# A recurrence with its products evicted to borrowed tiles, its second to fourth operand sets loaded earlier, and a new step order

## The chip, the cores and the metric

The kernel runs on one core of a Trainium2 chip. Its time is the device time of one execution in microseconds (us); below, the median of three runs. A profiled execution gives the trace. The engines are TensorE (PE in the profile; PEld are its weight loads), VectorE (DVE), ScalarE (ACT), GpSimd (POOL) and SyncE (SP), which issues most DMA transfers.

## The reference

Inputs r, k, v, w, a, b of 4 batches, 8 heads, 768 steps, 40 features run through a recurrence; its output is the input of two further layers.

```
for t in range(S):
    y[t]  = r[t] @ state
    Sa    = state @ a[t]
    state = state * w[t] - outer(Sa, b[t]) + outer(v[t], k[t])
u   = x + ((x^T @ U) @ V)^T;  x = u + relu(u @ w_ch1) @ w_ch2      (320 -> 1280 -> 320)
out = top-2 of 4 causal attention heads of width 64, each weighted by its gate, @ wo
```

## The kernel before

The recurrence (L58 to L486, the first 372.6 us) works on 12 chunks of 64 steps and 2 pairs of batches: 24 units u, unit u = chunk u // 2, pair u % 2. Operands come in 16 sets j of 1.05 MB (128 rows of 2057 floats: 512 columns each of two key-like factors and of a, and 521 of w). Two sets (j = 2m, 2m + 1) hold three units: set 2m + r holds unit 3m + r in 80 of its rows, and half of unit 3m + 2, the guest, in the 40 other rows that are used. The slots of sets 0 and 1 are tiles of their own (ldt), those of sets 2 and 3 lie in not yet used parts of the output tiles (x).

The order of the work on all engines is written out by hand: ORDER_R is a string, each letter runs one generator up to its next yield (L477). Each engine works through its own instructions in that order; semaphores do the rest. The letters:

- d, scaled(j): VectorE makes the scans P (L195) and er (L203), the product bkt (L208) and F (L216); then SyncE issues unit u's rows ga (L219), two transfers. Four steps a set.
- g, sent(j): three pairs of transfers by SyncE (L164), which bring the guest's rows of P, bkt and F into P_g, bkt_g and the guest's ga. P_g and bkt_g exist once.
- m, loads (L177): one load of a set, or of a piece; before, sets 1 to 3 come in three pieces (a, b, c).
- f, front(u): TensorE transposes P (pt) and bkt (pb) and multiplies bkt by ga (pg, L255, two halves); ScalarE evicts. The halves of pg are evicted over bkt itself (L258), so the eviction waits for every reader of bkt. Then GpSimd copies four blocks into lx (L263), cuts masks into ga (sel, L266) and copies m21 (L270).
- l, lanes(g): after every fourth unit VectorE inverts 32x32 triangles of lx: a transpose (lt, L279), 60 small instructions (L285, L288) and a transpose to tf (L297). Each d step and each later VectorE step also advances it by one.
- A, B, core(u) for even and odd units: TensorE and ScalarE solve with ga, tf, m21 and update the state st (L362, L364). They need tf of their group of four.
- p, q, outs(u): output products pn (L403), masks (L396, VectorE), py (L416, L420) and the last product (L426).
- y: the first loads of vin and rin; z: zeroing by GpSimd; u: the weights of the next layer, converted in ldt (L542 to L550), the next load issued one step ahead (L602); x: products pux (L666), two matmuls a step over 12 steps, each two records in the trace.

WAIT = (a, b, c) says how many letters later the mask (a), the last product (b) and the state update (c) are queued after the matmuls that they read. Behind the recurrence come the channel mix and the attention, in their own fixed orders.

Of the kernel before, what the change touches and what calls it, by code (L numbers as in the profile page):

```python
# [11 lines left out]
F32 = mybir.dt.float32  # L12
# [12 lines left out]
C = 64  # L25
# [3 lines left out]
PP = 8  # L29
# [10 lines left out]

WAIT = (2, 3, 3)
ORDER_R = (
    'zddlllllldllllmgdlmgdlzfdldlglfmfgfzdgfdmfllyfgmlfffmfdfdfmmddllfflglmlgdffddgdglgllffldzl',
    'ffglldllllmlllfzylflllldflllflylfffldllflgldflflglffldlggylllfllgdmBffllAfflflflfffgAldlll',
    'BlmdlllfdfBgABAfqBAllfqlqBAddlgllldgmpdpldBlgllAqpgllfBAlffBAqfqqfpBAppflgllldddllffBmlffl',
    'qplfllqfqldpdlglflAlqffflBAgqplBdAgBlAfpqBpAplmlldldlfgdllgpqqBllllAflfglplAlBpfplAlBllAfl',
    'llfqBpfAmBqgqpdAlflldqlldlllllflffplqqgBlddfflllpplglfmlAdBggfdqllfpBABAflpllqBllplqlfddll',
    'glflqlfdfplBlfflmdpgqABfpfqlqldfABpABpplAllgfAqgBldqmAlfpdfdlplglffgBgllfplfddlfqllpffAfdl',  # L50
    'lgfqlqlAfllflllmlllBlAfABppABpgqfBqlqAddppfgllAllBlqdqllpdfggBlqlqldffAlBgAlBfpAqlpqBlffll',
    'ffflfllpflflfllpulpqAlBplAqlqBAllulqBllAlpqBpAxBlqlllxlllAlppqllxxlBAlllqulpBAqlqlBlABplpl',
    'AllppBxqllllqlllllAqlllpBplqqlABullplqBAllBAlpqplquBAllpqlpxxllluBApqpBlAqqlBAlluBAlqqppAq',
    'qpxlllullxxqppqllpqulplqlBplllxxllx',
)


def recurrence(ctx, tc, ld, vin, rv, ident, xs, keep, wpool, mix):  # L58
# [29 lines left out]
    tfs = [const.tile([128, 32, 32], F32, name=f"tf{i}") for i in range(2)]  # L88

    ldx = [x[:, NC // 3:].rearrange("p c f -> p (c f)")[:, :LDW] for x in xs]  # L90
    guests = [fpool.tile([128, PP, CW], F32, name="P_g"), fpool.tile([128, PP, 2, C], F32, name="bkt_g")]
    nc.gpsimd.memset(guests[0], 1.0)
    nc.gpsimd.memset(guests[1], 0.0)

    def slot(j):
        return (ldt + ldx)[j % 4 if j < 6 else j % 2]

    mix.spare = lambda: fpool.tile([128, 2 * (S // 4)], F32, tag="lx", name="spare")
    BK, GA, PC, LX, M21, TF, UP = {}, {}, {}, {}, {}, {}, {}

    def load_ld(j, a=0, b=LDW):
        nc.sync.dma_start(slot(j)[:, a:b], ld[j, :, a:b])

    def load_v(u):
        c, bp = divmod(u, NBP)
# [60 lines left out]
    def sent(j):  # L166

        m, r = divmod(j, 2)
        f3 = slot(j)[:, :3 * PP * C].rearrange("p (k q t) -> p k q t", k=3, t=C)
        away(guests[0], PF[3 * m + r], r)  # L170
        yield
        away(guests[1], BKT[3 * m + r], r)
        yield
        away(GA[3 * m + 2][:, r], f3[:, 2], r)
        yield

    def loads():  # L177
        for j in range(1, NSET):
            for y in parts[j == 1:] if j < 4 else ((0, LDW),):
                load_ld(j, *y)  # L180
                yield

    def scaled(j):

# [38 lines left out]
    def front(u):  # L223

        g, uu = divmod(u, GU)
        c, bp = divmod(u, NBP)
        P, early = PF[u], u < GU
        pc = PC[u] = const.tile([128, PP], F32, tag="pc", bufs=16, name=f"pc{u}")
        nc.scalar.activation(pc, P[:, :, C], AF.Copy)
        pt = ps.tile([128, 4, 2, D], F32, tag="f", bufs=3, name=f"pt{u}")  # L230
        for p in range(4):
            for b in range(2):
                nc.tensor.matmul(pt[64 * b:64 * b + 64, p], P[:, 2 * p + b, :C],
                                 ident.rearrange("p (r e) -> p r e", r=2)[:, :, :D], start=True, stop=True)
        nc.scalar.activation(xs[bp][:, c], pt.rearrange("p a r d -> p (a r d)"), AF.Copy)
        yield

        bkt = BKT[u]
        BK[u] = wpool.tile([128, PP, 2, D], F32, tag="bk", bufs=AHEAD + 4, name=f"bk{u}")
        for h in range(2):  # L240
            pb = ps.tile([128, HP, 128], F32, tag="f", bufs=3, name=f"pb{u}_{h}")
            for p in range(HP):
                nc.tensor.transpose(pb[:, p], bkt[:, h * HP + p].rearrange("p k t -> p (k t)"), ident)
            nc.scalar.activation(BK[u][:, h * HP:h * HP + HP],
                                                 pb.rearrange("p q (r e) -> p q r e", r=2)[:, :, :, :D], AF.Copy)
            yield

        ga = GA[u]
        m21 = M21[u] = const.tile([128, PP, 32], F32, tag="m21", bufs=AHEAD + 1, name=f"m21{u}")
        if uu == 0:  # L250
            LX[g] = fpool.tile([128, 32, 32], F32, tag="lx", name=f"lx{g}")
        for h in range(2):
            pg = ps.tile([128, HP, 2, C], F32, tag="o" if early else "f", bufs=3, name=f"pg{u}_{h}")
            for p in range(HP):
                nc.tensor.matmul(pg[:, p], bkt[:, h * HP + p].rearrange("p k t -> p (k t)"),  # L255
                                 ga[:, :, h * HP + p], start=True, stop=True)
            hs = slice(h * HP, h * HP + HP)
            nc.scalar.activation(bkt[:, hs], pg, AF.Copy)  # L258
            if h:
                for r in range(2):  # L260
                    for i in range(2):
                        q = slice(64 * r + 32 * i, 64 * r + 32 * i + 32)
                        nc.gpsimd.tensor_copy(LX[g][q, uu * PP:uu * PP + PP], bkt[q, :, r, 32 * i:32 * i + 32])  # L263
                for r in range(2):
                    z = slice(64 - 64 * r, 128 - 64 * r)
                    nc.gpsimd.affine_select(ga[z, r], bkt[z, :, r], [[0, PP], [1, C]], OP.is_gt, 0.0, base=0,  # L266
                                            channel_multiplier=-1)
                for r in range(2):
                    q = slice(64 * r, 64 * r + 32)
                    nc.gpsimd.tensor_copy(m21[q], bkt[q, :, r, 32:])  # L270
            if h and uu == GU - 1:
                LN.append(lanes(g))
            yield

    def lanes(g):

# [164 lines left out]
    def fronts():  # L441
        for v in range(NU):
            yield from front(v)
# [18 lines left out]
            yield  # L462

    parts = (n, LDW), (0, 2 * PP * C), (2 * PP * C, n)
    for a, b in parts:
        load_ld(0, a, b)
    load_ld(1, *parts[0])
    for u in (0, 2, 1):
        blank(u)
    engines = mybir.EngineType  # L470
    ctx.enter_context(tc.manual_schedule(engines={engines.PE, engines.DVE, engines.Activation, engines.Pool, engines.SP}))
    units = [range(bp, NU, NBP) for bp in range(NBP)]
    seqs = {"A": chain(*[core(u) for u in units[0]]), "B": chain(*[core(u) for u in units[1]]),
            "p": chain(*[outs(u) for u in units[0]]), "q": chain(*[outs(u) for u in units[1]]),
            "d": chain(*[scaled(j) for j in range(NSET)]),
            "g": chain(*[sent(j) for j in range(NSET)]), "m": loads(), "y": firsts(), "f": fronts(), "z": ready(), "l": more(),
            "u": mix.weights(mix.sources()[0], ldt, (guests[0].rearrange("p q t -> p (q t)"), hot)),  # L477
            "x": mix.products(ps)}
    for x in "".join(ORDER_R):
# [570 lines left out]
```

## Time and profile before

| | |
|---|---|
| median of 3 runs | 858.09 us (856.68 to 860.68) |
| the profiled execution | 858.54 us, span 856.8 us |
| TensorE busy | 780.3 us, 91% of the span |
| VectorE | 579.5 us, 68% |
| ScalarE | 469.9 us, 55% |
| GpSimd | 323.9 us, 38% |
| mean granted clock of TensorE | 0.97 |

The span runs from the first instruction to the last one. Busy times are sums over an engine's instructions; a busy TensorE is not one at its peak. A row of the timeline reads: start, duration, engine, line, operation, output<-input, count, and in brackets the idle time of the engine before it with what ended it. Where an instruction waits for several things, the one named came last by the trace.

### The profile page before, as it was taken

The numbers are of one execution on the slowest core, as the hardware profiler recorded it, in microseconds if no ns is written. First come the engines' busy times: TensorE is split into PE (matmuls) and PEld (weight loads), VectorE is DVE, ScalarE is ACT, GpSimd is POOL, SyncE is SP. The second block draws the span as 40 slices with busy tenths as digits, with TensorE's granted clock in tenths as the row PEclk, the third lists the DMA queues.
The fourth block names the chain that finished last, engine by engine and source line by source line (L and its number), as shares of the span: only waits on it lengthen the run. The fifth ranks groups of instructions, "written<-read, shape, count | busy, mean of one in ns | idle before, by whom it ended". The sixth has DMA issues, their size and how long they took to land.

```text
span 856.8 us, 22703 instructions
## 1 busy us (share of the span) xinstructions
PE 780.3 (91%) x9100; PEld 666.2 (78%) x9100; DVE 579.5 (68%) x1388; ACT 469.9 (55%) x1125; POOL 323.9 (38%) x456
## 2 busy tenths in 40 slices
PE   5666989989999897989899999999999999999997
PEld 4555888988898687877678888887778788887875
DVE  6599999988998997448624131322268868778773
ACT  3534867766677678723323231312168757767672
POOL 5664464536545324315513220202027344244430
PEclk9787999998999999899999999999999999999999
DMA  5554256555545364512100100000000010000101
GB/s 166 171 143 158 78 171 164 151 144 150 137 144 145 87 171 114 130 54 83 47 1 25 34 2 1 1 1 0 1 1 2 1 47 2 16 32 2 47 2 47
DMA packets 53201, 61.47 MB, mean 72 GB/s; under 512 B 31208, under 2 KB 38376, under 8 KB 51560
## 3 DMA queue, kind: packets, MB, share of 16 engines
q1 hardware_dynamic: 53096, 60.02, 24.6%
q8 instruction: 72, 1.18, 0.6%
q14 instruction: 33, 0.27, 0.1%
HBM read 47.46 MB, written 4.13 MB: 60 GB/s over the span
## 4 chain that ended last, share of the span: by engine, by line
PE 54%; DVE 19%; DMA 6%; issue 5%; ACT 4%; POOL 2%; SPq 1%; DVEq 0%; POOLq 0%; ACTq 0%
PE po L943 4%; PE ph L743 3%; PE pa L760 3%; PE ph L740 3%; PE pa L761 3%; PE pa L762 3%; PE ph L741 3%; PE ph L739 3%; PE tp L930 3%; DVE lt L288 3%; DVE tmp L285 3%; PE pn L403 2%; PE pw L343 2%; PE ps L890 2%; PE ps L889 2%
## 5 line engine op out<-in xcount | busy, mean ns | idle before, releaser
L913 POOL TENSOR_TENSOR P<-P,sm 128x128 f32<-128x128 f32 (+2 forms) x92 | 82.9, 931 | 127.6 <-DVE sm L903 115.4
L747 DVE SCALAR_TENSOR_TENSOR hl<-ph,hh 128x512 fp32r<-128x512 f32 x60 | 41.1, 690 | 118.6 <-ACT hh L746 116.1
L746 ACT ACTIVATE hh<-ph 128x512 fp32r<-128x512 f32 x60 | 35.1, 594 | 108.5 <-PE pa L762 101.2
L894 ACT ACTIVATE P<-ps,mx 128x640 f32<-128x640 f32 (+4 forms) x96 | 60.5, 634 | 26.1 <-DVE mx L892 18.1
L285 DVE TENSOR_TENSOR tmp<-lt 128x30 f32<-128x30 f32 (+9 forms) x180 | 70.3, 390 | 3.9
L288 DVE TENSOR_TENSOR lt<-lt,tmp 128x30 f32<-128x30 f32 (+9 forms) x180 | 69.0, 384 | 3.7
L892 DVE CUSTOM_DVE_ANT_0 ps<-ps,neg 128x640 f32<-128x640 f32 (+4 forms) x96 | 59.0, 639 | 7.6 <-PE ps L890 6.5
L263 POOL COPY lx<-bkt 32x256 f32<-32x256 f32 x64 | 30.0, 469 | 87.9 <-ACT bkt L258 85.8
L403 PE MATMUL pn<-rbd,uvt 128*128 128x128 f32 x384 | 54.9, 293 | 7.3 <-DMA uvt<-in_rin 5.7
L776 POOL TENSOR_TENSOR t<-t,ul 128x512 f32<-128x512 f32 x12 | 15.4, 1294 | 116.8 <-DVE t L775 116.7
L255 PE MATMUL pg<-ga,bkt 128*128 128x128 f32 x256 | 40.1, 318 | 19.6 <-DMA ga<-ldt 14.3
L403 PEld LDWEIGHTS pn<-rbd,uvt 128*128 128x128 f32 x384 | 49.6, 204 | 9.5 <-issue 4.9
L930 PE MATMUL tp<-ident,P 128*128 128x128 f32 x336 | 52.0, 276 | 1.8 <-ACT pt L934 0.8
L255 PEld LDWEIGHTS pg<-ga,bkt 128*128 128x128 f32 x256 | 36.6, 226 | 21.6 <-issue 12.7
L346 ACT ACTIVATE uv<-pw 32x320 f32<-32x320 f32 x96 | 41.1, 428 | 18.4 <-PE pw L343 16.7
L739 PE MATMUL ph<-uh,w 128*128 128x512 f32 x120 | 47.1, 399 | 1.7 <-ACT uh L728 1.6
L740 PE MATMUL ph<-ul,w 128*128 128x512 f32 x120 | 47.7, 397 | 0.6 <-DVE ul L729 0.6
L741 PE MATMUL ph<-uh,w 128*128 128x512 f32 x120 | 47.3, 396 | 0.0
L761 PE MATMUL pa<-hl,w 128*128 128x512 f32 x120 | 47.1, 392 | 0.0
L930 PEld LDWEIGHTS tp<-ident,P 128*128 128x128 f32 x336 | 39.4, 140 | 9.2 <-POOL P L913 2.7
L943 PE MATMUL po<-pt,vals 128*64 128x256 f32 (+3 forms) x320 | 45.1, 397 | 1.4 <-DVE o L959 1.0
L762 PE MATMUL pa<-hh,w 128*128 128x512 f32 x120 | 46.2, 391 | 0.0
(217 smaller groups left out, 2239.8 us busy)
## 6 DMA issues: line engine op xcount, KB each, us to landing
ldt<-in_ld SPq DMA_DIRECT2D x12, 1028.5 KB
uvt<-in_rin SPq DMA_DIRECT2D x48, 128.0 KB
rpt<-in_rin SPq DMA_DIRECT2D x24, 256.0 KB
rbd<-in_rin SPq DMA_DIRECT2D x48, 96.0 KB
uv<-in_vin SPq DMA_DIRECT2D x48, 80.0 KB
out<-o SPq DMA_DIRECT2D x24, 160.0 KB
ga<-ldt SPq DMA_DIRECT2D x28, 80.0 KB
room<-in_w SPq DMA_DIRECT2D x7, 320.0 KB
```

What stands on the lines that cost most here:

```text
L255: nc.tensor.matmul(pg[:, p], bkt[:, h * HP + p].rearrange("p k t -> p (k t)"), ga[:, :, h * HP + p], start=True, stop=True)
L285: nc.vector.tensor_tensor(tv, L[:, s + 1:, s:s + 1].to_broadcast([128, n, s]), L[:, s:s + 1, :s].to_broadcast([128, n, s]), op=OP.mult)
L288: nc.vector.tensor_tensor(L[:, s + 1:, :s], L[:, s + 1:, :s], tv, op=OP.add)
L403: nc.tensor.matmul(pn[h][:, p], ut[:, h * HP + p].rearrange("p r t -> p (r t)"), rbd[u % 2][:, :, h * HP + p], start=True, stop=True)
L739: nc.tensor.matmul(ph, w[:, 0, f], uh[:, ft], start=ft == 0, stop=False)
L740: nc.tensor.matmul(ph, w[:, 0, f], ul[:, ft], start=False, stop=False)
L741: nc.tensor.matmul(ph, w[:, 1, f], uh[:, ft], start=False, stop=False)
L761: nc.tensor.matmul(pa[ft], w[:, o:o + m], hl, start=False, stop=False)
L762: nc.tensor.matmul(pa[ft], w[:, 2 * DM - FT[2][0] + o:2 * DM - FT[2][0] + o + m], hh, start=False, stop=last)
L913: nc.gpsimd.tensor_tensor(p, p, sm[:, i:i + 1].to_broadcast([128, w]), op=OP.mult)
L930: nc.tensor.transpose(pt[:, j - j0], P[:, c:c + 128], ident)
L943: nc.tensor.matmul(po[64 * r:64 * r + 64, s0:w], VS[b][:, j, HD * e:HD * e + HD], PT[r][:, j, s0:], start=j == 0, stop=j == i1 - 1, skip_g ...
```

## The change

Units 0 to 3 evict pg to rbd[0], rbd[1], uvt[0], uvt[1], which are used later. The masks and m21 are a step of their own (letter k). Sets 0 and 1 are loaded in three pieces each before the ordered part, set 2 in two pieces by ScalarE, sets 3 to 15 in one piece by letter m. ORDER_R is a new string and WAIT is (1, 0, 0). Counted in the strings: they have 845 letters before and 871 after. Before the transpose of the first lanes step stand d of sets 0 to 3 and half of set 4 in the old string, three quarters of set 4 in the new one. The fifth lanes result (tf4), the last one (tf5) and the first u stand at letters 644, 741 and 646 in the old string, 658, 750 and 752 in the new one; the later u at 663, 703, 752, 770, 784, 800, 816 and at 762, 784, 796, 804, 818, 829, 847.

```
-WAIT = (2, 3, 3)
+WAIT = (1, 0, 0)
 ORDER_R = (
-    'zddlllllldllllmgdlmgdlzfdldlglfmfgfzdgfdmfllyfgmlfffmfdfdfmmddllfflglmlgdffddgdglgllffldzl',
-    'ffglldllllmlllfzylflllldflllflylfffldllflgldflflglffldlggylllfllgdmBffllAfflflflfffgAldlll',
...
+    'ddflldzdllldzddgmlgdfgfllfdlzlzlgdgfdfllgmdflkfdfffflkfffddlfllgflylgflddflllldlgffggdzgfl',
...
+    rooms = [t.rearrange("p r q t -> p (r q t)").rearrange("p (q r t) -> p q r t", q=PP, r=2) for t in rbd] + uvt
...
-    def load_ld(j, a=0, b=LDW):
-        nc.sync.dma_start(slot(j)[:, a:b], ld[j, :, a:b])
+    def load_ld(j, a=0, b=LDW, queue=nc.sync):
+        queue.dma_start(slot(j)[:, a:b], ld[j, :, a:b])
...
     def loads():
-        for j in range(1, NSET):
-            for y in parts[j == 1:] if j < 4 else ((0, LDW),):
-                load_ld(j, *y)
-                yield
+        for j in range(3, NSET):
+            load_ld(j)
+            yield
...
-            nc.scalar.activation(bkt[:, hs], pg, AF.Copy)
+            gm = GM[u] = rooms[u] if early else bkt
+            nc.scalar.activation(gm[:, hs], pg, AF.Copy)
...
+    def kept(u):
+
+        ga, gm = GA[u], GM[u]
+        m21 = M21[u] = const.tile([128, PP, 32], F32, tag="m21", bufs=AHEAD + 1, name=f"m21{u}")
+        for r in range(2):
+            z = slice(64 - 64 * r, 128 - 64 * r)
+            nc.gpsimd.affine_select(ga[z, r], gm[z, :, r], [[0, PP], [1, C]], OP.is_gt, 0.0, base=0,
+                                    channel_multiplier=-1)
+        for r in range(2):
+            q = slice(64 * r, 64 * r + 32)
+            nc.gpsimd.tensor_copy(m21[q], gm[q, :, r, 32:])
+        yield
...
-    for a, b in parts:
-        load_ld(0, a, b)
-    load_ld(1, *parts[0])
+    for j in range(2):
+        for a, b in parts:
+            load_ld(j, a, b)
...
+    for a, b in (parts[0], (0, n)):
+        load_ld(2, a, b, nc.scalar)
...
+            "k": chain(*[kept(u) for u in range(NU)]), "z": ready(), "l": more(),
```

## Rows read from the trace of the kernel before

**Rows 1.** Windows: stretch, length, busy us (instructions) by engine, clock, DMA share, GB/s

```profile
0.00:41.57 41.57, 23.27 (x190) 20.89 (x191) 24.16 (x32) 17.22 (x34) 24.73 (x49) 0.91 0.55 172
41.57:77.80 36.23, 21.06 (x220) 18.91 (x219) 34.07 (x77) 12.61 (x29) 18.57 (x35) 0.77 0.55 151
77.80:269.80 192.00, 177.62 (x4064) 166.85 (x4064) 179.94 (x394) 138.18 (x348) 97.72 (x158) 0.96 0.49 140
269.80:324.02 54.22, 47.26 (x1068) 41.13 (x1068) 49.28 (x120) 39.89 (x103) 19.77 (x35) 0.97 0.54 140
324.02:372.60 48.58, 43.97 (x962) 39.19 (x963) 27.26 (x53) 32.97 (x81) 18.29 (x23) 0.93 0.46 119
```

**Rows 2.** Waits of VectorE, 0 to 41.57 us: total us, times, longest

```profile
DVE bkt L208 <- DMA x<-in_ld: 4.0, 1, 4.0
DVE P L195 <- DMA ldt<-in_ld: 3.7, 2, 3.1
DVE P L195 <- PE pt L233: 2.7, 1, 2.7
DVE x L216 <- DMA x<-in_ld: 1.2, 1, 1.2
```

**Rows 3.** Timeline, 0 to 60 us, work of the first units

```profile
5.58 0.21 ACT L229 ACTIVATE pc<-P 128x8 f32<-128x8 f32 x1 [2.42 <-DVE P L195]
...
12.16 3.78 PE L255 MATMUL pg<-ga,bkt 128*128 128x128 f32 x16 [1.81 <-DMA ga<-ldt]
...
26.74 3.25 PE L255 MATMUL pg<-ga,bkt_g 128*128 128x128 f32 x16 [3.72 <-DMA ga<-ldt]
...
38.70 1.09 ACT L258 ACTIVATE bkt<-pg 128x512 f32<-128x512 f32 x2 [5.31 <-DMA bkt_g<-bkt]
...
39.84 1.69 POOL L263 COPY lx<-bkt 32x256 f32<-32x256 f32 x4 [2.11 <-ACT bkt L258]
...
41.57 1.97 DVE L279 STREAM_TRANSPOSE lt<-lx 128x1024 f32<-128x1024 f32 x1 [2.76 <-POOL lx L263]
...
43.77 1.23 DVE L208 TENSOR_TENSOR bkt<-ldt 128x1024 f32<-128x1024 f32 x1
```

**Rows 4.** Timeline of SyncE's issues, 0 to 60 us

```profile
8.96 1.56 SPq L219 DMA_DIRECT2D ga<-ldt  x2
...
13.91 0.57 SPq L102 DMA_DIRECT2D x<-in_ld  x1
...
20.91 1.40 SPq L164 DMA_DIRECT2D ga<-ldt  x2
22.35 3.13 SPq L102 DMA_DIRECT2D x<-in_ld  x4
...
35.45 1.36 SPq L164 DMA_DIRECT2D bkt_g<-bkt  x2
```

**Rows 5.** DMA view, 0 to 11 us in 40 slices

```profile
GB/s 0 0 0 0 0 0 68 144 159 129 76 249 375 455 357 447 387 402 350 390 348 288 435 455 432 372 403 166 68 53 0 0 0 0 0 0 0 60 209 30
```

**Rows 6.** Lines of VectorE, 269 to 324.02 us: count, busy, mean ns, idle before

```profile
L543 DVE SCALAR_TENSOR_TENSOR ldt<-ldt 128x512 int32<-128x512 int32 (+1 forms) x3 | 2.4, 799 | 0.1
L547 DVE SCALAR_TENSOR_TENSOR ldt<-ldt 128x512 f32<-128x512 uint32 (+1 forms) x3 | 2.0, 670 | 0.1
...
L546 DVE TENSOR_SCALAR ldt<-ldt 128x512 int32<-128x512 int32 (+1 forms) x3 | 1.6, 517 | 0.1
L542 DVE TENSOR_SCALAR ldt<-ldt 128x512 int32<-128x512 int32 (+1 forms) x3 | 1.5, 497 | 2.7 <-DMA ldt<-in_v 2.6
```

**Rows 7.** Timeline, 334.5 to 342 us, products and a weight load

```profile
335.69 1.30 PE L666 MATMUL pux<-x,u 128*64 128x320 f32 x8
...
337.07 0.54 SPq L602 DMA_DIRECT2D ldt<-in_w  x1
...
341.10 0.33 DVE L542 TENSOR_SCALAR ldt<-ldt 128x320 int32<-128x320 int32 x1 [2.95 <-DMA ldt<-in_w]
```

**Rows 8.** Waits of VectorE, 77.8 to 372.6 us

```profile
DVE uvt L396 <- PE pn L403: 10.3, 7, 2.0
DVE st L362 <- PE pw L357: 3.7, 3, 2.8
```

More of the change, by code (lines that the diff above doesn't have):

```diff
@@ L37 @@
 NSET = 2 * NU // 3
-WAIT = (2, 3, 3)
+WAIT = (1, 0, 0)
 ORDER_R = (
-    'zddlllllldllllmgdlmgdlzfdldlglfmfgfzdgfdmfllyfgmlfffmfdfdfmmddllfflglmlgdffddgdglgllffldzl',
-    'ffglldllllmlllfzylflllldflllflylfffldllflgldflflglffldlggylllfllgdmBffllAfflflflfffgAldlll',
[L47 to L54, printed above, removed]
+    'ddflldzdllldzddgmlgdfgfllfdlzlzlgdgfdfllgmdflkfdfflflkfffddlfllgflylgflddflllldlgffggdzgfl',
+    'dllflfllklllfllllklllfflAflllkflmflllllfflgykdglldfldgfflgllffyldBlllkfgfffflflmfBglddlkAl',
+    'lflgldfyBlAllBAlkfqlBlqAqmllBpAldqdBfplpggABdfmgddllAglflfflplfAqqklBAfdgfqlBllpfqfllpflBm',
+    'lllflqllldplkpglflAqllllddfBlApplkBlABAfqdglpBgfAqllmlpfpdgldqAdlBllfflpqglfBgqfllflpdAllB',
+    'lfklAlBAqlflpBAplqqfqlmpllBlkfAldlldlfldpllffkqfqlplflgggdpllfgBAllddlmffApfBlAppdgBqlfplp',
+    'llABqdfdflflqlfglmllAqkllpqdBqgfdkffAllpfBqfdldfkBgAgBgldqgqfqlffAldBpplflllfqfBllApqlkllm',
+    'llfllpAdplfflBAfdfgfqlllAlkBAfBpAdmlklpppplABfqqlldAdlggBqgqABdpqAdlfldBflgfpBffglgAfllqBl',
+    'qlllplllflfqqflllfpllflflqlllffllpllBlllAlpllqBAplBABlAqpBlqAplppqllkllkAlpqllBplqqllllABp',
+    'lllqlllllABlABppqlllqpqllBlAlklpuBlpAqlqlBulAqpBAlBlAxxBqlAlxlxxulllBqpApqllullqxqlpuxxBlp',
+    'lllqpABlupApAqlpllBulllplpBlxqxplqlpqulllqqlplullpAlqllqxxllx',
 )
@@ L98, in recurrence @@
     mix.spare = lambda: fpool.tile([128, 2 * (S // 4)], F32, tag="lx", name="spare")
-    BK, GA, PC, LX, M21, TF, UP = {}, {}, {}, {}, {}, {}, {}
-    def load_ld(j, a=0, b=LDW):
-        nc.sync.dma_start(slot(j)[:, a:b], ld[j, :, a:b])
+    BK, GA, GM, PC, LX, M21, TF, UP = {}, {}, {}, {}, {}, {}, {}, {}
+    def load_ld(j, a=0, b=LDW, queue=nc.sync):
+        queue.dma_start(slot(j)[:, a:b], ld[j, :, a:b])
     def load_v(u):
@@ L248, in front @@
         ga = GA[u]
-        m21 = M21[u] = const.tile([128, PP, 32], F32, tag="m21", bufs=AHEAD + 1, name=f"m21{u}")
         if uu == 0:
@@ L262, in front @@
                         q = slice(64 * r + 32 * i, 64 * r + 32 * i + 32)
[L263 to L270, printed above, removed]
+                        nc.gpsimd.tensor_copy(LX[g][q, uu * PP:uu * PP + PP], gm[q, :, r, 32 * i:32 * i + 32])
             if h and uu == GU - 1:
@@ L475, in recurrence @@
             "d": chain(*[scaled(j) for j in range(NSET)]),
-            "g": chain(*[sent(j) for j in range(NSET)]), "m": loads(), "y": firsts(), "f": fronts(), "z": ready(), "l": more(),
+            "g": chain(*[sent(j) for j in range(NSET)]), "m": loads(), "y": firsts(), "f": fronts(),
+            "k": chain(*[kept(u) for u in range(NU)]), "z": ready(), "l": more(),
             "u": mix.weights(mix.sources()[0], ldt, (guests[0].rearrange("p q t -> p (q t)"), hot)),
```

## The prediction

> **What bounds the kernel now.** The profile is read by stage first: the windows [rows 1], cut where the first lanes step starts (41.57), where its result is there (77.80), at the first weight load (269.80), at the last lanes result (324.02) and at the end of the recurrence (372.60). From 77.80 to 324.02 VectorE is busy 94 and 91%, TensorE 93 and 87%: neither has much to give, and the stage moves as a whole with its start. From 324.02 to 372.60 TensorE alone is near full. In the first 41.57 us VectorE is busy 24.16 only, so 17.4 us are idle. Next come the waits of VectorE in that stretch [rows 2]: 4.0, 3.7, 2.7 and 1.2 us, 11.6 in all, end with a transfer of operands (the 2.7 is put down to a product that reads another tile; the scan behind it reads a piece of set 2 that SyncE issued at 13.91 [rows 4], so I count it as a load too). Last the chain in front of the first lanes step [rows 3]: unit 3's eviction waits 5.31 us for a transfer that reads the tile it overwrites, GpSimd's copies wait for the eviction, and VectorE waits 2.76 us for the copies. That transfer stands at 35.45 [rows 4], behind GpSimd's last read of the guest tile.
>
> **Part 1, the first four evictions go to other tiles.** The same eight ScalarE instructions, nothing added. The 5.31 us [rows 3] go for units 1 and 3, since nothing is read from the new tiles by a DMA. The tiles are operands of steps that stand much later in the order (letters 133 and 187; the last reader of the four stands at 107), so I cost the loan at nothing; without that gap the zeroing of rbd and the first operand loads would wait for GpSimd's reads.
>
> **Part 2, the loads.** Sets 0 and 1 are issued before everything, set 2 by ScalarE in two instructions, set 3 as the fifth issue after the first guest rows, in one piece instead of three. ScalarE's two issues cost about 0.6 us each by SyncE's single issue [rows 4], and fit into the 2.42 us that ScalarE waits before its first real work [rows 3]; uncovered they would delay only the first pc. With the loads ahead the 11.6 us of rows 2 can go. What is late next is SyncE's queue. By the new order it issues nine pairs and two set loads from F of set 0 (8.96) to unit 3's rows. A pair takes 1.36 to 1.56 and a single 0.57 [rows 4], so the last, unit 3's rows, are out at 8.96 + 9 x 1.4 + 2 x 0.57 = 22.7. From there to the product that reads them the trace has 1.6 us (out at 10.52, product at 12.16) and 4.4 (out at 22.31, product at 26.74, with 1.3 MB of loads on the queue) [rows 3, 4]. Set 4's 1.05 MB stand right before, so I take 4.4: 27.1. Two products take 2.0 to 3.8 us (3.78 at 12.16, 3.25 at 26.74) [rows 3]; I take 2.6 as TensorE has no gaps in front; an eviction is 0.55 and the four copies 1.69 [rows 3]: the lanes start at about 32.0. VectorE is not later: it had 24.16 us of work before its first lanes step, and the new order puts one product more before it (bkt of set 4, 1.23 [rows 3]), 25.4 us, plus some 2 us in which it waits for the first load: 28 is its floor. So the lanes start between 28 (floor) and 41.5 (the old chain); I take 32.3, near the queue's sum. VectorE then is 41.57 - 32.3 + 1.2 = 10.5 us ahead, and all up to 269.80 moves with it, since behind the first lanes step both strings have the same further VectorE work up to its result (set 4's F, all of set 5). Bounds: 1.2 to 14.8.
>
> A rule speaks against this part. The row of transferred bytes [rows 5] shows 350 to 455 GB/s from one queue from 3.3 to 7.2 us, while the first sets land; at 400 a set of 1.05 MB takes 2.6 us. The Trainium skill ("DMA: Bandwidth & Descriptors", section "Issuing engines are not separate DMA queues") says that transfers started by different engines run on the same 16 DMA engines and interleave, so a second issuing engine saves only issue time. By that rule set 2 takes its 2.6 us out of what lands beside it, set 1 and the first units' rows; if all of that reached the lanes the time would be 848.6 instead of 846.0. No run here has two issuing queues, so it stays open.
>
> **Part 3, the masks as own steps.** The same four GpSimd instructions a unit, later: units 0 to 3's copies into lx no longer stand behind them. Who waits for them are the units' own cores (69 or more letters later for units 0 to 3) and, from unit 4 on, the tile's next writer on VectorE and SyncE's next guest rows, with all that is queued behind them. In the new string these stand 9 or more letters behind, but for unit 15 (5) and unit 17 (2). GpSimd is busy 51% there [rows 1], so I take nothing; bounds +3 (two waits of about the 1.69 of four copies [rows 3]) and -2 (the copies of units 1 to 3 no longer behind masks).
>
> **Part 4, the order behind.** The new string puts the conversion of the mix weights (letter u, eight of them) and the products x behind the last lanes result; the old one has three conversions and five products before it. Moved out of the stage 269.80 to 324.02: 2.4 + 2.0 + 1.6 + 1.5 = 7.5 us of VectorE and a wait of 2.7 [rows 6], and of TensorE five steps of products, 20 records at 1.30 us for eight [rows 7], 3.3 us. TensorE keeps 47.26 - 3.3 = 44.0, and at the 92.5% of the stage before (177.62 of 192.00 [rows 1]) that needs 47.5: -6.7 (VectorE, 41.8 at 93.7%, would need 44.6). The last stage gets the 3.3 us: at its 90.5% +3.6. VectorE there goes from 27.26 to 34.8 of 48.58, which doesn't bind; but the conversions wait for loads, 2.95 us once in five before [rows 7], so for eight 4.7: +1.8, of which I take 1. Net -2.1; bounds -10.2 (all of VectorE's share, tail hidden) and +20 (below). The shorter WAIT, (1, 0, 0) for (2, 3, 3), queues masks, state updates and the final product closer behind the matmuls that they read. VectorE waits for such matmuls 10.3 + 3.7 us from 77.80 on [rows 8]; since their letters were placed anew too, I take no change, bounds -7 and +7 (half of it).
>
> **The sum**, against the profiled execution's own 858.54 (span 856.8 and 1.7 around it): 858.5 - 10.5 - 2.1 = 845.9, so 846. The median of the runs shown, 858.09, is 0.45 lower, within their spread.
>
> **The rivals.** (a) The queue stays the limit: the pairs on SyncE wait for each other as before (the guest tiles are still single, and still passed from one pair of sets to the next), and unit 3's copies come as late as 39.84 [rows 3]. Then only the 1.2 and part 4 are left: 855. For it: before, the waits between those issues took longer than the issues [rows 4]. Against: what they waited for were set loads and the mask copies, both moved away. (b) VectorE's floor: rows land 1.6 us after issue, the lanes start at 28, 14.8 are won, and part 4 gives 6.7 with the tail hidden: 837. Against it stands set 4's load in front of unit 3's rows. (c) The queue distance: half of rows 8 again as new waits, 7 us: 853. (d) Slower: the tail. All eight conversions stand on VectorE in front of masks and state updates that TensorE needs, and each waits for its load, since only two rooms exist and a load is issued one step ahead. If each of eight waited 2.95 [rows 7], 23.6 instead of 3.0: +20.6, less the 1 already counted: 866. It turns the gain over once a conversion waits 2.1 us on average (12.6 + 1 + 3.0 = 16.6 over eight). Against it: the gaps between these letters are 8 to 22; with some 53 us for the 121 letters behind the last lanes result, 0.44 each, 8 are 3.5 us, and issue to use took 4.0 (337.07 to 341.10 [rows 7]), so most would wait little.
>
> **How the numbers follow.** Forecast 0.52, (a) 0.12, (b) 0.12, (c) 0.14, (d) 0.10. The range 837 to 856 holds the forecast with its terms off by 4 to 9 us, (a), (b) and (c), and leaves out (d) and the ends: about 0.82. About 0.5%, 4.3 us, is what a measurement of this kernel tells from no change. Faster: forecast, (b) and half of (c), 0.71; same: (a) and the other half of (c), 0.19; slower: (d), 0.10.
>
> **What would show it.** Right: no wait of ScalarE for bkt_g before the first lanes step; VectorE's load waits in rows 2 under 3 us together; the first lanes step at 30 to 35; its result near 67; stage 4 shorter by some 6 us and the last stage longer by 4 to 5. Wrong: the first lanes step past 38, with SyncE's pairs or unit 3's rows as releaser (a); the same step early but the distance lost by 270, with waits for pn and pw grown (c); conversions waiting for ldt over 2 us each behind the last lanes result (d). The forecast falls if the lead at the first lanes result is not still there at the last one.

## The result, and the profile of the changed kernel

The changed kernel takes 862.65 us (median; 856.58 to 869.88), the kernel before 857.49 beside it: a ratio of 1.0066, interval 1.0043 to 1.0089. It is slower, by about 5 us; the forecast was 846, with a range of 837 to 856. Ratios and intervals compare executions run beside each other, without the few that were slow as a whole, so they need not be the quotient of the two medians (here 1.0060). Executions of one kernel spread by some 10 us: the changed one took 866.02 at a mean granted clock of 0.961 and 856.99 at 0.978. The profiled execution took 859.71 (span 858.0), 1.17 more than that of before (858.54); so the two traces below differ by 1.2 us where the medians differ by 5.

Windows of the changed kernel: stretch, length, busy us (instructions) of PE, PEld, DVE, ACT and POOL, granted clock, DMA share, GB/s. The cuts are the start of the first lanes step, the transposes that give the first, fifth and last lanes result, and the end of the last product:

```profile
0.00:36.38 36.38, 22.08 (x210) 19.79 (x212) 25.60 (x34) 18.36 (x35) 24.68 (x45) 1.00 0.64 200
36.38:71.84 35.46, 17.71 (x197) 16.08 (x192) 33.27 (x74) 9.87 (x23) 19.88 (x34) 0.71 0.42 105
71.84:276.85 205.01, 187.66 (x4155) 173.14 (x4152) 183.36 (x406) 146.93 (x371) 96.48 (x166) 0.97 0.51 141
276.85:313.67 36.82, 34.39 (x925) 31.43 (x922) 35.18 (x89) 27.32 (x71) 10.79 (x23) 1.00 0.41 106
313.67:372.51 58.84, 51.23 (x1013) 42.95 (x1013) 40.01 (x69) 37.93 (x93) 22.77 (x30) 0.89 0.53 138
```

The kernel before, cut at the same marks (finer than [rows 1]):

```profile
41.57:75.83 34.26, 19.96 (x212) 18.05 (x211) 32.10 (x76) 11.18 (x26) 16.87 (x30) 0.76 0.56 157
75.83:271.89 196.06, 180.18 (x4089) 169.17 (x4086) 183.68 (x407) 141.67 (x358) 100.30 (x165) 0.97 0.50 140
271.89:322.03 50.14, 44.85 (x1050) 38.91 (x1049) 45.53 (x106) 36.39 (x94) 17.99 (x31) 0.97 0.52 137
322.03:369.90 47.87, 42.26 (x950) 37.52 (x949) 28.13 (x51) 33.03 (x83) 19.18 (x25) 0.93 0.43 110
```

Read downward, the changed kernel gains 5.19 us to the first lanes step (41.57 to 36.38), loses 1.20 of them in that step (34.26 to 35.46), loses 8.95 from the first to the fifth lanes result (196.06 to 205.01), gains 2.35 from there to the last product (50.14 + 47.87 to 36.82 + 58.84), and 1.41 behind it (486.90 to 485.49). The sum is +1.2. From the first to the fifth lanes result VectorE does the same work (183.68 us in 407 instructions, 183.36 in 406), so the loss is idle time of VectorE: 12.4 us before, 21.7 after. The granted clock of the stretch is 0.97 in both, so it is not what makes the difference.

Of its waits there, first in the kernel before those for pw and pn, then in the changed kernel the three longest (total us, times, longest):

```profile
DVE st L362 <- PE pw L357: 3.5, 2, 2.8
...
DVE uvt L396 <- PE pn L403: 0.6, 1, 0.6
```

```profile
DVE uvt L402 <- PE pn L409: 5.1, 4, 1.8
DVE st L368 <- PE pw L363: 4.4, 1, 4.4
DVE lt L285 <- POOL lx L263: 2.2, 2, 1.9
```

In the kernel before the whole list holds 6.7 us, 4.1 of them behind TensorE's pn and pw, the products that the masks and state updates of [rows 8] read; in the changed kernel it holds 15.8, and 9.5 of them behind pn and pw.

TensorE, however, stands idle hardly longer. By these marks, which are VectorE's, it is busy 187.66 us in 4155 records where it was busy 180.18 in 4089, so its own idle time grows only from 15.9 to 17.4; behind the fifth lanes result, up to the last product, it has 1938 records instead of 2000. (A few per cent of the records can be missing.) So part of the 8.95 is work of TensorE that stood behind the fifth mark before. From the first lanes result to the last product the two traces take 294.07 and 300.67: 6.6 us lost, more than the lead of 4.0.

The head. Waits of VectorE up to the first lanes step of the changed kernel:

```profile
DVE bkt L208 <- DMA bkt_g<-bkt: 3.1, 1, 3.1
DVE lt L285 <- POOL lx L263: 2.9, 1, 2.9
DVE P L195 <- DMA ldt<-in_ld: 1.1, 1, 1.1
...
DVE P L195 <- DMA P_g<-P: 1.0, 1, 1.0
```

SyncE's issues there, first and last rows of units 0 and 3:

```profile
9.87 1.69 SPq L219 DMA_DIRECT2D ga<-ldt  x2
...
22.82 0.52 SPq L103 DMA_DIRECT2D ldt<-in_ld  x1
23.43 2.06 SPq L219 DMA_DIRECT2D ga<-x  x2
```

The timeline in front of the first lanes step, and ScalarE's first wait for bkt_g:

```profile
23.98 3.59 POOL L263 COPY lx<-rbd 32x256 f32<-32x256 f32 x4 [1.70 <-ACT rbd L258]
...
27.64 1.71 POOL L274 TENSOR_SCALAR_AFFINE_SELECT ga<-rbd 64x512 f32<-64x512 f32 x2
...
29.07 1.95 PE L254 MATMUL pg<-ga,bkt 128*128 128x128 f32 x16
29.30 1.77 POOL L278 COPY m<-rbd 32x256 f32<-32x256 f32 x2
30.43 1.22 ACT L258 ACTIVATE uvt<-pg 128x512 f32<-128x512 f32 x2
31.13 5.22 POOL L263 COPY lx<-uvt 32x256 f32<-32x256 f32 x8
...
36.38 2.00 DVE L285 STREAM_TRANSPOSE lt<-lx 128x1024 f32<-128x1024 f32 x1 [2.90 <-POOL lx L263]
...
54.30 1.08 ACT L258 ACTIVATE bkt<-pg 128x512 f32<-128x512 f32 x2 [10.50 <-DMA bkt_g<-bkt]
```

The load waits of [rows 2] are gone but for 1.1 us and one of 0.4, and so is ScalarE's 5.31 [rows 3]. In their place VectorE waits for transfers of guest rows (3.1 and 1.0), and for GpSimd, which works without a gap from 23.98 to 36.35 and is the last to arrive.

### The profile page after: what moved, and what is told of

The parts are those of the page before. It is cut to its first block, busy times and chain, and to the rows that moved or that the text cites. A ratio compares the mean times of both kernels' runs of the same rounds, so it can differ in the third digit from the quotient of the medians.

```text
span 858.0 us, 22658 instructions
## 1 busy us (share of the span) xinstructions
PE 781.5 (91%) x9100; PEld 664.1 (77%) x9100; DVE 584.5 (68%) x1388; ACT 470.7 (55%) x1125; POOL 321.2 (37%) x456
## 4 chain that ended last, share of the span: by engine, by line
PE 59%; DVE 15%; DMA 6%; ACT 6%; issue 5%; POOL 2%; SPq 2%; DVEq 0%; POOLq 0%; ACTq 0%
PE po L952 4%; PE tp L939 3%; PE pn L409 3%; PE pa L769 3%; PE ph L752 3%; PE pa L770 3%; PE pa L771 3%; PE ph L748 3%; PE ph L750 3%; PE ph L749 3%; DVE lt L294 2%; PE pw L325 2%; DVE tmp L291 2%; PE ps L899 2%; PE pg L254 2%
## 5 line engine op out<-in xcount | busy, mean ns | idle before, releaser
L294 DVE TENSOR_TENSOR lt<-lt,tmp 128x30 f32<-128x30 f32 (+9 forms) x180 | 72.0, 400 | 3.9
L263 POOL COPY lx<-bkt 32x256 f32<-32x256 f32 x52 | 24.3, 467 | 82.4 <-ACT bkt L258 80.6
L254 PE MATMUL pg<-ga,bkt 128*128 128x128 f32 x256 | 37.9, 305 | 13.4 <-DMA ga<-ldt 12.7
```

The costliest lines, as they stand in the source:

```text
L294: nc.vector.tensor_tensor(L[:, s + 1:, :s], L[:, s + 1:, :s], tv, op=OP.add)
```

## The experiments

NEW and OLD are the two order strings; K(a, b) puts the masks of units a to b - 1 directly behind their copies, as before, and drops their letters k. "New head, old order" is what the expectations call e1_new_head_old_rest, or e1. Ratios are to the kernel before, run beside each kernel. The marks are from one profiled execution each; the last product's is its end.

| run | lanes start | first result | fifth | last product | ratio (interval) |
|---|---|---|---|---|---|
| before | 41.57 | 75.83 | 271.89 | 369.90 | 1 |
| after | 36.38 | 71.84 | 276.85 | 372.51 | 1.0066 (1.0043 to 1.0089) |
| new head, old order | 36.41 | 71.92 | 268.65 | 364.60 | 0.993 (0.990 to 0.9959) |
| the same again | 36.28 | 71.77 | 267.62 | 365.59 | 0.9935 (0.9903 to 0.9966) |
| old head, new order | 41.75 | 76.14 | 277.60 | 372.11 | 1.004 (1.0008 to 1.0073) |
| loads alone | 44.74 | 79.14 | 270.93 | 366.59 | 1.006 (1.002 to 1.010) |
| evictions alone | 40.55 | 74.69 | 269.62 | 366.65 | 0.9987 (0.996 to 1.0015) |
| masks in place | 38.20 | 71.23 | 277.78 | 379.35 | 1.006 (1.0027 to 1.0094) |
| masks behind copies | 34.64 | 70.60 | 268.00 | 366.25 | 0.9942 (0.9909 to 0.9975) |
| load behind rows | 36.35 | 71.87 | 276.82 | 373.94 | 1.0038 (1.0009 to 1.0067) |
| short WAIT | 36.32 | 71.78 | 276.26 | 379.73 | 1.0103 (1.0066 to 1.014) |
| WAIT (3, 4, 4) | 36.73 | 72.20 | 263.85 | 363.46 | 0.9996 (0.9965 to 1.0028) |
| WAIT (1, 3, 3) | 36.64 | 72.12 | 266.62 | 363.75 | 1.0006 (0.9972 to 1.0039) |
| WAIT (2, 0, 3) | 36.53 | 72.01 | 270.47 | 369.79 | 1.0007 (0.9976 to 1.0037) |
| WAIT (2, 3, 0) | 36.31 | 71.81 | 268.87 | 365.80 | 1.0024 (0.999 to 1.0059) |
| new order, WAIT (2, 1, 3) | 36.20 | 71.67 | 278.40 | 380.87 | 1.0126 (1.0088 to 1.0165) |
| conversions late | 36.14 | 71.65 | 266.74 | 377.55 | 1.0065 (1.004 to 1.0089) |
| conversions early | 36.15 | 71.60 | 279.91 | 395.74 | 1.0276 (1.0233 to 1.0319) |
| new tail on old order | 36.25 | 71.72 | 267.93 | 366.94 | 1.000 (0.997 to 1.003) |
| old tail on new order | 36.35 | 71.81 | 278.76 | 381.58 | 1.0072 (1.0038 to 1.0106) |

**Which half loses.** The new head with the old order behind the first lanes result, and the opposite:

```
-WAIT = (1, 0, 0)
+WAIT = (2, 3, 3)
-ORDER_R = NEW
+ORDER_R = NEW[:175] + "yk" + OLD[177:]     # its first B an A; K(8, 24)
```

> The changed kernel up to the first lanes result (early loads, evictions to other tiles, new string up to there, masks of units 0 to 6 as own steps), and from there the string, the WAIT and the masks' place of the kernel before. Theory 1 (the lead of 4 us that the trace of after has at the first lanes result is real, and the new string behind it loses it): 853.5, 0.995 of before; first lanes result at about 72, from there to the end of the products about 294 as before. Theory 2 (the early part itself costs later, since TensorE stands idle at 40 to 60 us, its granted clock falls, and GpSimd's backlog is handed on): 861 to 863 as after, with some 5 us more between the first and the second lanes result.

```
+ORDER_R = OLD[:177] + NEW[175:]     # its first A a B, one y and one k an l; K(0, 8)
...
-            gm = GM[u] = rooms[u] if early else bkt
+            gm = GM[u] = bkt
...
-    for j in range(2):
-        for a, b in parts:
-            load_ld(j, a, b)
+    for a, b in parts:
+        load_ld(0, a, b)
+    load_ld(1, *parts[0])
...
-    for a, b in (parts[0], (0, n)):
-        load_ld(2, a, b, nc.scalar)
```

> The mirror: loads, evictions and string of before up to the first lanes result, then the string, the WAIT and the masks as own steps of after. Theory 1: the loss without the lead, 866, 1.010 of before; first lanes result at 76, the second one some 52 us later. Theory 2: no loss, since the early part is the old one: 855 to 858.

852.0 and 861.32 us, ratios 0.993 and 1.004. The first is theory 1; the second lies between its two theories, 855 to 858 and 866. The head is a gain in front of the old order, and the new order a small loss behind the old head. The two do not add up: 0.993 times 1.004 is 0.997, and the changed kernel, which has both, is at 1.0066. The marks say why. With the old head the new order's fifth lanes result stands at 277.60, with the new head at 276.85: nearly the same, though the lanes start 5.4 us apart. From the first lanes result to the last product it takes 295.97 behind the old head, 1.9 more than the kernel before, and 300.67 behind the new one. So most of what the changed kernel loses there is the lead itself, which the new order does not use. What it includes, letters, WAIT and the masks' place, is taken apart below. The first kernel, run once more with the last group:

> The new head with the old order and its WAIT (2, 3, 3) behind it, unchanged, beside the two mixed orders of this group. Theory 1 (the lead of the head is carried to the end): ratio to the kernel before 0.990 to 0.996 again. Theory 2 (the runs with one distance shortened, all near 1.0, say that the first measurement was a lucky one): 0.997 to 1.001.

853.15 us, 0.9935: the gain holds.

**Parts of the head.** The loads alone, and the evictions alone, each in the kernel before:

```
-    for a, b in parts:
-        load_ld(0, a, b)
-    load_ld(1, *parts[0])
+    for j in range(2):
+        for a, b in parts:
+            load_ld(j, a, b)
...
+    for a, b in (parts[0], (0, n)):
+        load_ld(2, a, b, nc.scalar)     # m letters 2 to 8 of OLD become z
```

> The kernel before with the new loads alone: sets 0 to 2 ahead, set 2 by ScalarE, set 3 at the old place of set 1's second piece. VectorE's 11.6 us of load waits go, but unit 3's eviction still waits for the guest rows behind GpSimd's masks. If the loads carry most of the lead: lanes start at 37 to 39, 854. If the evictions must come with them: 40 or later, 857 to 858.

```
-            nc.scalar.activation(bkt[:, hs], pg, AF.Copy)
+            gm = GM[u] = rooms[u] if early else bkt
+            nc.scalar.activation(gm[:, hs], pg, AF.Copy)     # the copies and masks read gm; K(0, 24)
```

> The kernel before with the first four evictions to rbd and uvt alone, loads and string unchanged. The 5.31 us wait of unit 3's eviction goes; if its chain sets the lanes: start at 36 to 37, 853 to 854. If the late loads hold VectorE anyway: 40, 857.

859.59 (1.006) and 852.84 (0.9987; its median alone would give 0.9946, so a small gain is not excluded). By the start of the lanes the second expectation holds for both. In the old string the loads make the first lanes step 3.2 us later, and the evictions make it 1.0 earlier. With the loads alone VectorE's waits up to the lanes are:

```profile
DVE bkt L208 <- POOL m L281: 7.8, 2, 5.8
DVE lt L288 <- POOL lx L263: 6.9, 1, 6.9
DVE P L195 <- DMA ldt<-in_ld: 2.3, 2, 1.3
```

The load waits are nearly gone, and waits for GpSimd stand in their place: VectorE writes the next bkt where GpSimd still reads the evicted pg of an earlier unit. (The z letters in the place of m bring GpSimd's zeroing forward, to 3.3 to 11.0 us, well before its first copy at 20.76.) So neither part gives the 5.2 alone; both together in the old string were not run, so what the letters of the new head add is open.

In the new head with the old order, the masks of units 0 and 1 behind unit 3's copies:

```
-ORDER_R = NEW[:175] + "yk" + OLD[177:]
+ORDER_R = ...     # the first two k moved behind unit 3's last f
```

> e1_new_head_old_rest with the masks of units 0 and 1 (two letters k) moved behind the copies of unit 3. In the trace of after GpSimd works without a gap from 23.98 to 36.35, 3.5 us of it on the masks of unit 1, and VectorE waits 2.90 us for its copies. If GpSimd is what sets the first lanes step: 3 to 5 us earlier than 36.4, first lanes result at 68, time 847 to 850, 0.989 of before. If the rows of unit 3 set it (the forecast's term): no earlier than 35.5 and 852.

GpSimd's copies in that run:

```profile
23.68 4.02 POOL L263 COPY lx<-rbd 32x256 f32<-32x256 f32 x4 [4.37 <-ACT rbd L258]
...
27.85 1.70 POOL L263 COPY lx<-uvt 32x256 f32<-32x256 f32 x4 [0.15 <-ACT uvt L258]
31.64 2.97 POOL L263 COPY lx<-uvt 32x256 f32<-32x256 f32 x4 [2.09 <-ACT uvt L258]
```

The first lanes step comes at 34.64, 1.8 us before the 36.41 of the same kernel without the move, so those masks did stand in its chain; now unit 3's eviction is waited for (2.09). The lead is 1.3 us at the first lanes result and nothing at the end (852.97, 0.9942).

**The place of the masks, and of a load.** In the changed kernel, K(0, 24); and the load of set 8 behind unit 10's rows:

```
+            if h:
+                for _ in kept(u):
+                    pass     # in front(), behind the copies; letter k does nothing
```

> The changed kernel, but every unit's masks directly behind its copies into lx as before (the letter k does nothing). If the masks' later place is what costs (guest rows and evictions that wait for GpSimd: 10.5 us of ScalarE at 54): 857 to 859, and that wait under 5. If it costs nothing: 862 to 863. If the copies of units 1 to 3 profit from it: the first lanes step 2 us later than 36.4, and 864.

```
-ORDER_R = NEW
+ORDER_R = NEW[:226] + NEW[227:230] + "m" + NEW[230:]
```

> The changed kernel with one letter m (the load of set 8, 1.05 MB) moved from in front of unit 10's rows to right behind them. In the trace of after these rows land 5.2 us after their issue, TensorE stands 3.9 us before the product that reads them, a state product is queued behind it, and VectorE waits 4.4 us for that. If this is the loss between the first and the second lanes result: that stage 48 to 49.5 instead of 52.7, time 858 to 860. If not: 862 to 863 and the stage over 51.

864.45 (1.006) and 861.83 (1.0038). With the masks in place the first lanes step is 1.8 us later, at 38.20, and the time the same within the intervals. With the load moved the stage takes 52.43; the wait of 4.4 for the state product is gone, and VectorE waits 4.7 for pn instead. Neither brings the loss back, though the second leaves room for 1 or 2 us.

**The distance.** WAIT is counted in letters. In the new head with the old order:

```
-WAIT = (2, 3, 3)
+WAIT = (1, 0, 0)
```

> e1_new_head_old_rest with WAIT (1, 0, 0) for (2, 3, 3). If the short distance loses the lead of after (rival c of the prediction): 856 to 860, VectorE's waits for pw, pn and py up by 5 us or more. If it doesn't, since the letters around it decide: 850 to 853.

866.51, 1.0103: 14 us lost by the distance alone, more than either expectation, and some 8 of them before the fifth lanes result. Windows from the first to the fifth lanes result, first of the new head with the old order (its second run), then with the short WAIT, then VectorE's wait for pw in the first and its longest waits in the second:

```profile
71.77:267.62 195.85, 180.35 (x4096) 169.69 (x4094) 183.83 (x407) 142.57 (x358) 102.38 (x165) 0.96 0.53 146
```

```profile
71.78:276.26 204.48, 181.21 (x4071) 170.25 (x4069) 181.74 (x407) 141.03 (x354) 97.10 (x162) 0.95 0.49 140
```

```profile
DVE st L371 <- PE pw L366: 0.3, 1, 0.3
```

```profile
DVE st L371 <- PE pw L366: 6.9, 5, 3.0
DVE P L195 <- issue: 3.3, 1, 3.3
DVE uvt L405 <- PE pn L412: 2.9, 2, 2.5
DVE x L435 <- PE py L429: 2.6, 3, 1.6
```

VectorE's work is the same to about 1% in both, and TensorE's to 0.5%; what grows most is VectorE's waiting for pw, the product that the state update reads, from 0.3 to 6.9 us. Longer, then each of the three alone shorter:

```
-WAIT = (2, 3, 3)
+WAIT = (3, 4, 4)
```

> e1_new_head_old_rest with WAIT (3, 4, 4). The short one cost 14 us there. If VectorE still stands in front of unfinished products (its 14.5 us for pn and 4.3 for py in e1): 848 to 851. If the masks then come late for TensorE: 855 or more.

```
-WAIT = (2, 3, 3)
+WAIT = (1, 3, 3)
```

> The new head with the old order behind it (852.0, ratio 0.993), with WAIT (1, 3, 3) for (2, 3, 3): only the masks of pn are queued one letter closer. WAIT (1, 0, 0) cost it 14 us. Theory 1 (each distance has its share): 3 to 5 us, 855 to 857, ratio 0.996 to 1.0. Theory 2 (the masks, which have the longest waits, carry it): 8 or more, 860, ratio 1.003.

```
-WAIT = (2, 3, 3)
+WAIT = (2, 0, 3)
```

> The new head with the old order, with WAIT (2, 0, 3) for (2, 3, 3): only the last products' multiplication by the gate is queued at once. In the run with WAIT (1, 0, 0) VectorE's waits for py grew by 5.1 us. Theory 1 (each its share): 4 to 6 us, 856 to 858, ratio 0.998 to 1.0. Theory 2 (one of the other two carries it): 852, ratio 0.993.

```
-WAIT = (2, 3, 3)
+WAIT = (2, 3, 0)
```

> The new head with the old order, with WAIT (2, 3, 0) for (2, 3, 3): only the state update is queued at once behind the matmuls that it reads. In the run with WAIT (1, 0, 0) VectorE's waits for pw grew by 6.1 us. Theory 1 (each its share): 4 to 7 us, 856 to 859, ratio 0.998 to 1.001. Theory 2 (one of the other two carries it): 852, ratio 0.993.

856.05, 856.18, 857.86 and 858.53, ratios 0.9996 to 1.0024: each puts the old order 0.7 to 0.9% behind its (2, 3, 3) at 0.993, the longer one too. Each of these differences is uncertain by about 0.4%, and for (3, 4, 4) the interval touches that of the repeat (0.9903 to 0.9966). For the single distances that is "each its share". Their profiled executions don't show where: those of (1, 3, 3) and (2, 3, 0) are the fastest of their runs (851.15 and 851.96), with last products at 363.75 and 365.80, and that of (3, 4, 4) has the earliest fifth lanes result of all, 263.85.

The opposite, in the changed kernel. (2, 3, 3) does not go with the new string: a product x would stand before the final multiplication of the output that it reads, so there is no time for that kernel. (2, 1, 3) is near it, with a shorter middle distance:

```
-WAIT = (1, 0, 0)
+WAIT = (2, 1, 3)
```

> The changed kernel with WAIT (2, 1, 3) for (1, 0, 0), nothing else. Theory 1 (the short distance is what the new order loses by): some 7 to 12 us come back, 851 to 856, ratio to the kernel before 0.99 to 1.0. Theory 2 (the new order was fitted to its own distance): no gain, 860 to 870, ratio 1.003 to 1.015.

867.08, 1.0126, four executions: theory 2. The fifth lanes result is no earlier (278.40), and the waits between stay:

```profile
DVE uvt L402 <- PE pn L409: 5.2, 4, 2.8
DVE st L368 <- PE pw L363: 2.9, 2, 2.1
```

So a short distance is enough to cost the old order this much, but a longer one gives the new order nothing back. That the new order loses by its WAIT is therefore not shown.

**Conversions and products.** Late in the old order, early in the new one (u and x spread as in the other string):

```
-ORDER_R = NEW[:175] + "yk" + OLD[177:]
+ORDER_R = ...     # the same, u and x behind the last lanes result as in NEW; z, idle there, in their old places
```

> e1_new_head_old_rest with all conversions and products (letters u and x) behind the last lanes result, spread there as in the new string. Part 4 of the prediction (the stage before loses 6.7, the last one gains 4.6): 850, last lanes result 6 to 10 us earlier. Rival d (the conversions hold VectorE in front of masks and state updates): 856 or more, with the last stage longer by 10 or more, as in after (58.8 instead of 47.9).

```
-ORDER_R = NEW
+ORDER_R = ...     # the same, u and x spread as in OLD; z, idle there, in their old places
```

> The changed kernel with the conversions and products (letters u and x) spread as in the old string: three u and five x ahead of the last lanes result. If the tail is what loses in the changed kernel too (it does on e1: +11.5 us): 852 to 856, last stage 48 to 51 instead of 58.8, the last lanes result 5 to 8 us later. If part 4 of the prediction holds for the string that was written for it: 864 or more.

863.98 (1.0065) and 878.83 (1.0276). In the first the last lanes result comes 9 us earlier, as part 4 of the prediction had it, but the stage behind it takes 69.0 instead of 47.0; late conversions wait for their loads as rival (d) had it,

```profile
DVE ldt L554 <- DMA ldt<-in_w: 12.7, 3, 10.2
```

with one wait of 10.2, and the old order loses 12 us by the move. The second is "864 or more", by a wide margin: the new order loses 16 more with early conversions. Moving these letters alone between strings loses both ways. Moving all letters behind the fifth lanes result instead:

```
-ORDER_R = NEW[:175] + "yk" + OLD[177:]
+ORDER_R = ...     # up to the fifth lanes result; from there what is left, in the sequence of NEW
```

> The new head and the old order up to the fifth lanes result, from there on the letters in the sequence of the new string (conversions and products late), with WAIT (2, 3, 3); the last x letters are two places later. From the fifth lanes result to the last product the changed kernel takes 95.7 us and the old order on the new head 96.0. Theory 1 (the new tail is as good as the old one, the loss lies between the first and the fifth lanes result): last product near 364.5, as the new head with the old order, ratio 0.993 to 0.998. Theory 2 (the tail only fits its own distance and what stands before it): 8 us or more later, ratio 1.002 or more.

```
-ORDER_R = NEW
+ORDER_R = ...     # up to the fifth lanes result; from there what is left, in the sequence of OLD; K(21, 24)
```

> The changed kernel up to the fifth lanes result, from there on the letters in the sequence of the old string (conversions and products early), with WAIT (1, 0, 0); masks as own steps for units 0 to 20. Theory 1 (the loss lies before the fifth lanes result): last product near 373, as the changed kernel, 862, ratio 1.006. Theory 2 (the old tail loses with the short distance: 103.4 us there in the run of the old order with WAIT (1, 0, 0)): last product near 380, 870, ratio 1.014.

857.17 (1.000) and 866.69 (1.0072). The first lies between its theories: the new tail takes 99.0 us on the old order, against 96.0 and 98.0 for the old one, with the last product at 366.94; by the timed runs it is 0.65% behind the old tail. So the new tail costs the old order something, but less than the 8 us of theory 2. The old tail with the short WAIT takes 102.8, near theory 2 by the mark and near theory 1 by the ratio. The fifth lanes result stands at 278.76 again: in all seven executions with the new order on either head it lies between 276.8 and 279.9, in the nine with the new head and the old order at a WAIT with at most one distance shortened, between 263.9 and 270.5.

## Why the prediction was wrong

By its own steps, against 845.9:

**Part 1** was right: ScalarE's first wait for bkt_g comes behind the first lanes step, at 54.30.

**Part 2** had the sign and half the size. The forecast start of the lanes was 32.3, it is 36.38. SyncE's queue was the right account of the rows, and too short. Its first issue of rows is at 9.87, not 8.96 [rows 4]: set 0's operands land later, with set 2 from ScalarE and two more pieces of set 1 from SyncE beside them. (With the loads alone it is at 9.76.) The rule in the Trainium skill ("DMA: Bandwidth & Descriptors", section "Issuing engines are not separate DMA queues") has transfers of different engines interleave on the same 16 DMA engines. The sign of the 0.9 us agrees with it, and the size is below the 2.6 of my estimate; how much of it is set 2's, no run separates. (The row of bytes that the 2.6 rests on dips to 288 once within the 350 to 455; 400 is near its mean.) The nine pairs take 1.32 to 2.06, 13.6 in all where I had 12.6, with 0.9 between them, so the rows of unit 3 are out at 25.49 (23.43 + 2.06) and not 22.7; their product starts at 29.07 and not 27.1: 2.0 us. The masks of unit 1 and its m21 (27.64 to 31.07) stand before the copies of units 2 and 3; moving them gave 1.8. My sum took a unit's four copies at 1.69 us [rows 3]; those of unit 1 took 3.59 beside VectorE's scans, and those of units 2 and 3, which come last, 5.22 together. Rival (a) was wrong: SyncE's pairs follow each other almost without a gap.

The lanes' start of 36.38 lies between the sign for "right" (30 to 35) and that for (a) (past 38). The lead at the first lanes result is 4.0 us rather than 10.5: 5.2, not the 9.3 of the start (41.57 to 32.3), and 1.2 lost in the lanes, where I had 1.2 won. VectorE has two instructions fewer there and is busy 1.17 us longer, beside a GpSimd that is busy 19.88 us rather than 16.87.

**Part 3** was right where it said that later masks cost nothing (masks in place: 1.006 against 1.0066), and wrong in passing over the two letters k before the first lanes step.

**Part 4** came near its net by luck, through other terms: -2.35 from the fifth lanes result to the last product, where I had -2.1, but as -13.3 and +11.0 rather than -6.7 and +4.6 (my cut was at 269.80 and 324.02, here 271.89 and 322.03). In the last stage VectorE's waits of the changed kernel are:

```profile
DVE ldt L551 <- DMA ldt<-in_w: 6.8, 3, 3.8
DVE uvt L402 <- PE pn L409: 4.0, 3, 2.5
```

6.8 us for the loads of conversions, where I had 4.7, so rival (d) did not decide this kernel. The old order with late conversions is where it showed.

**The step that failed** is "all up to 269.80 moves with it". It does with the old order behind the new head (0.993 and 0.9935), and does not with the new order: 8.95 us lost between the first and the fifth lanes result by VectorE's marks, 6.6 up to the last product, more than the whole lead of 4.0. Behind the old head the same order loses 1.9, so it is above all the lead that it does not pass on. The condition that the lead must still be there at the last lanes result was the right place to look, and the sign set for (c) came, "the distance lost by 270, with waits for pn and pw grown". Of the 9.3 us that VectorE idles longer, 5.4 stand behind pn and pw; at 853 rival (c) had this too small on top of too large a lead. Whether the shorter WAIT ("I take no change") is part of it is not shown: it costs the old order 14 us, and a longer one gives the new order nothing back. I read the new string for what moved (conversions, products, masks, loads) and took the rest as equal because it has the same letters: 238 of TensorE against 239 in this stretch. Equal in number, they need not be equal in distance to what waits for them; that this is the reason is an argument, which no run here tests.

The terms add up: +6.5 (lead 4.0, not 10.5), +9.0 (the middle), -0.3 (part 4) and -1.4 (behind the last product, not forecast) are 13.8, and 845.9 + 13.8 = 859.7, the profiled execution. The median is 2.9 us above it.

What is not settled: which letters of the new order between its first and fifth lanes result carry the loss, and what holds its fifth result at 277 to 280 whatever the start. The masks' place and the one load tried do not, and a longer WAIT does not undo it. The loss also moves within the stretch: with the same letters up to the fifth result, the stage from the fourth to the fifth took 46.83 us in the changed kernel and 54.55 with the old tail (where the masks of units 21 and 22 stand in it too). Its windows in the two, and then two pieces of the second:

```profile
230.02:276.85 46.83, 45.17 (x1055) 42.06 (x1053) 42.83 (x99) 36.43 (x94) 19.49 (x35) 1.00 0.49 130
```

```profile
224.21:278.76 54.55, 51.12 (x1065) 47.43 (x1066) 44.62 (x100) 37.85 (x98) 23.25 (x43) 0.91 0.44 117
246.00:256.30 10.30, 10.30 (x156) 9.50 (x154) 5.44 (x12) 5.16 (x14) 1.84 (x3) 0.54 0.43 106
256.30:266.50 10.20, 10.20 (x234) 9.52 (x234) 8.21 (x18) 7.46 (x18) 3.09 (x6) 1.00 0.24 62
```

TensorE does nearly the same work in both; in the second its granted clock is 0.54 from 246.00 to 256.30, almost all of it at the lower level of 1.2 GHz, right behind 2.50 us in which it stood idle. Fully busy, it gets through 156 records there, and through 234, of not quite the same mix, in the next 10.20 us at 2.4 GHz. From the first to the second lanes result it is the other way round: 52.74 us at 0.90 in the changed kernel, 48.48 at 0.96 with the old tail. So where in the stretch the loss shows goes with where the clock falls; over the whole stretch the clock is 0.97 in the kernel before and in the changed one.

Of all kernels run, the new head with the old order and WAIT (2, 3, 3) is the fastest, 0.7% ahead of the kernel before and, by the two ratios, 1.4% ahead of the change (0.993 / 1.0066 = 0.986). With the masks of units 0 and 1 behind the copies (0.9942) it is the same within the intervals.

## What to carry to other kernels

A lead that is won at the start of an order written out by hand is worth only what the order behind it keeps: check the same marks along the whole run, and time the head with the old order behind it before judging it. Test the two halves crossed as well: here their effects did not add. Where two engines are both some 90% busy, the distances between an instruction and what it waits for are tuned together with the sequence: in the old order each of four changes of the distance alone cost 0.7 to 0.9%, shortening all three 1.7%, and none helped. Equal instruction counts in a stage say nothing on its waits. Marks on one engine do not cut another engine's work at the same place.

## What was not expected of the hardware

GpSimd's four copies into lx took 1.70 us while VectorE stood idle (27.85 in the run with the masks behind the copies), and 3.59 and 4.02 us beside VectorE's scans and products of some 1.2 us each. A scan of VectorE, 1.24 us alone, took 1.44 beside them in one case (24.55 in the changed kernel) and 1.24 in another (23.65 in the run with the masks behind the copies). The Trainium skill ("GPSIMD Engine Reference", section "1. Specifications") says that GpSimd's SBUF interfaces are shared with VectorE, with contention where a VectorE instruction reads two inputs from SBUF. The slow copies agree. But beside the lanes' products, which read two inputs too and take 0.4 us each, four copies took 1.70 again (at 43.08 in the changed kernel). A cost taken from a copy beside an idle engine was too low by a factor of 2.1 to 2.4 beside the long instructions.
